# Emission sorted by replayed time, and clock fillers on the spare columns of a score bank

## The chip, the core and the metric

The kernel runs on one core of one Trainium2 chip. The metric is the device time of one execution in microseconds (us), from the median of several runs. The core has five engines with a queue each: PE (TensorE, whose weight loads the profile lists as PEld), DVE (VectorE), ACT (ScalarE), POOL (GpSimd) and SP (SyncE, which issues the DMAs here). Each engine works through its own queue in order and waits on semaphores of the others.

## The reference

Thresholded attention over 8 batches and 8 heads (576 tokens, head dimension 64), then a two-layer feed-forward block over the 4608 tokens with a piecewise gate:

```python
scores = scale * np.matmul(q, k.transpose(0, 1, 3, 2))
thresh = np.max(scores, axis=-1, keepdims=True) - tau
scores = np.where(scores >= thresh, scores, -1000000000.0)
scores = scores - np.max(scores, axis=-1, keepdims=True)
attn = np.exp(scores)
attn = attn / (np.sum(attn, axis=-1, keepdims=True) + 1e-09)
attn_out = np.matmul(attn, v)
...
h = x @ w_in
g = np.where(pos, h, np.where(neg, 0.0, (h + beta) ** 2 / (4.0 * beta)))
return g @ w_out
```

`x` is the attention output with the heads side by side, `pos` is h >= 1 and `neg` is h <= -1.

## The kernel before, in words

All matrices are split into a high and a low float16 part, and a product is three matmuls (high x high, high x low, low x high).

The work falls into stages that overlap. The two weight matrices are loaded in 16 pieces each, and every piece is put together from bits on ACT, POOL and DVE (lines 760 to 787). PE squares each piece into the bank `acc` (the "gram" matmuls, line 794); DVE takes the largest value (line 705), PE spreads it over the partitions (line 708), DVE makes the scales (lines 455 to 457 and 713 to 718), and then the pieces are split into their two parts, some with the help of PE (the "conversions", lines 856 and 857, evicted by ACT at line 863 or DVE at line 861). For q and k, ACT takes sums of squares (line 540), PE spreads them (line 548), DVE and POOL make scales (lines 455 to 457, 555, 560) and the parts are written (lines 568 to 581). v of the first batch is turned by PE (line 679) into a score bank and split by ACT and DVE (lines 684 and 688).

A score tile is 128 rows of queries against 576 keys. PE writes it into one of two score tiles `s0`, `s1` (line 981). A score tile has two PSUM banks of 512 float32 columns; 288 columns of each hold scores, and one more a pad. DVE finds the extreme (line 998), ACT takes the exponential (line 1005), DVE masks and sums (line 1019; in the first tiles line 1025), POOL normalizes (line 1037), ACT and POOL write the two parts (lines 1042 and 1045), and a DMA turns them (line 1067). The first two tiles are turned by PE instead (line 1089, evicted by ACT and DVE at lines 1092 and 1095). PE then multiplies with v (line 1145), and ACT and DVE write the result to `x` (lines 1153 and 1157). The feed-forward block is line 1217 (into one of three banks `ph`), its gate on ACT and DVE (lines 1223 to 1240), line 1262 (into `acc`), and the eviction at line 1280.

The order of the work is a table. Every step is recorded as an operation with an engine, a cost, its predecessors and the buffers it takes and uses. `Plan.order` replays the operations in the order of the table `ORDER`, with those costs: an operation starts at the replayed time `o.t`, when its engine is free, its predecessors have ended and a buffer of its pool is free. The replay decides which slot of a pool each operation gets. The operations are then emitted one after another; emission appends the instructions to the queues of their engines, and the framework adds a semaphore wait wherever an instruction touches a tile region or a PSUM bank that an instruction emitted earlier still reads or writes.

Fillers are matmuls of `ones` with `ones` (128 x 128) whose result nobody reads. They are meant for PE's gaps in the replay, up to 200 us of replayed time, in number `WARM[2]` (0.6) of the gap over `WARM[3]` (0.056 us). Before the change, `gaps` walks over the PE operations in emission order. For each gap over `WARM[0]` it looks through the banks (three of `ph`, `acc`, two of `s`) for the one that stays unheld longest after the gap's start, and notes the gap's start, that bank and the length. The emission loop sets a group ahead of the first operation whose replayed time is not before the gap's start. That gives three groups, of 17, 29 and 19 fillers (line 1296), all on `ph` banks.

Of the kernel before, what the change touches and what calls it, by code (L numbers as in the profile page):

```python
# [18 lines left out]
P = 128  # L19
# [10 lines left out]


EXPM = 0x7F000000
WARM = (1.0, 200, 0.6, 0.056)

LOAD, WLOAD = (0.82, 0.75, 1.8), (1.3, 1.28, 2.0)
QMOVE, KMOVE = (0.33, 0.33, 1.35), (0.64, 0.62, 1.35)
# [243 lines left out]
class Plan:  # L280
# [38 lines left out]
    def order(self):  # L319

        free = {p: [(0.0, x) for x in v] for p, v in self.free.items()}
        idle, dma, mode, self.held = dict.fromkeys(self.HOP, 0.0), 0.0, 0, []
        for o in self.ops:
            o.t = 0.0
        for o in (self.ops[n] for n in ORDER):
            t = max(o.t, idle[o.eng], dma - self.QUEUE if o.eng == "SP" else 0.0)
            for b in o.take:
                x = min(free[b.pool], key=lambda f: f[0])
                free[b.pool].remove(x)
                b.slot, b.end = x[1], 0.0  # L330
                t = max(t, x[0])
            o.t = t
            for b in o.take:
                b.since = t
            end = idle[o.eng] = t + o.cost + (self.TURN if o.eng == "PE" and o.mode != mode else 0.0)
            if o.eng == "PE":
                mode = o.mode
            if o.work:
                dma = max(dma + o.work[0], end + o.work[1])
                end = dma + o.work[2]  # L340
            if o.gives:
                free[o.gives[0]] += [(end + self.FREE, x) for x in o.gives[1]]
            for b in o.uses:
                b.users -= 1
                b.end = max(b.end, end)
                if not b.users:
                    free[b.pool].append((b.end + self.FREE, b.slot))
                    self.held.append((b.pool, b.slot, b.since, b.end))
            for x in o.next:
                x.t = max(x.t, end + (self.HOP[o.eng] if x.eng != o.eng else 0.0))  # L350
            for x in o.behind:
                x.t = max(x.t, t)
        return [self.ops[n] for n in ORDER]


@with_exitstack
def attn_ffn_kernel(ctx: ExitStack, tc: tile.TileContext, qT, kT, vT, tau, w_in, w_out, out):
# [21 lines left out]
    V, A, G, T, Y = nc.vector, nc.scalar, nc.gpsimd, nc.tensor, nc.sync  # L379

    plan = Plan()
# [8 lines left out]
    s_ps = [pp.tile([P, 2, 512], F32, name=f"s{i}") for i in range(2)]  # L390
    plan.pool("ph", 3)
    ph = [pp.tile([P, 512], F32, name=f"ph{i}") for i in range(3)]
    plan.pool("acc", 1)
    accs = [pp.tile([P, 512], F32, name="acc")]
# [32 lines left out]
    ones = cp.tile([P, P], BF16, name="ones")  # L427
# [503 lines left out]
    for b in range(B):  # L931
        s, f, wi, wo = scs[:, b, :], fcs[:, b], wsc["i"], wsc["o"]
# [248 lines left out]
    def wide(g):  # L1181
        return g >= WIDE and len(groups[g]) == 1
# [4 lines left out]
    for g, c0 in [(g, c0) for g in range(NG) for c0 in range(0, gtok[g], GN if wide(g) else P)]:  # L1187
        n = GN if wide(g) else P
# [5 lines left out]
        for fc in range(0, NFC, k):  # L1194
# [49 lines left out]
            o = plan.op("PE", 12 * k * (n / 2400 + 0.0027), ffn1, xdone[g, c0] + xdone.get((g, c0 + n - P), []) + wi, take=[hb, qs[1]], uses=[xbuf[g]])  # L1244
            o = plan.op("ACT", 0.685 + 0.295 * (m - 1), relu, [o] + [fscale[b] for b in bs], take=[tb], uses=[hb])
            o = plan.op("ACT", 0.525, square, [o], uses=[tb])
            o = plan.op("DVE", 0.665 + 0.263 * (m - 1), gate, [o], uses=[tb, hb])
            o = plan.op("ACT", 0.718 + 0.285 * (m - 1), ghi, [o], take=[qs[0]], uses=[hb, qs[1]])
            o = plan.op("DVE", 0.788 + 0.248 * (m - 1), glo, [o], uses=[hb, *qs])
            steps.append((fc, qs, gv, [o] + wo))  # L1250
        for t0 in range(0, n, P):
            if t0:
                ab = plan.buf("acc")
            head, o, left = None, [], [len(steps)]
# [27 lines left out]
            o = plan.op("ACT", 0.575, evict, o + [mo] + [oscale[b] for b in bs], take=[ob], uses=[ab])  # L1282
# [5 lines left out]

                plan.op("SP", 0.55, store, [o], uses=[ob], work=(0.68 * r / P, 0.65 * r / P, 1.05))

    banks = [("ph", x, t[:, :P]) for x, t in enumerate(ph)] + [("acc", 0, accs[0][:, :P])] + [("s", x, t[:, 1, :P]) for x, t in enumerate(s_ps)]

    def keep_warm(bank, us):

        for _ in range(int(us / WARM[3])):
            T.matmul(bank, ones, ones, start=True, stop=True)

    def gaps(order):

        found, free = [], 6.0  # L1300
        for o in order:
            if o.eng != "PE":
                continue
            if o.t - free > WARM[0] and o.t < WARM[1]:
                best = max(((min([t0 for p, x, t0, t1 in plan.held if (p, x) == (pool, n) and t1 > free] + [o.t]), n, pool) for pool, n, _ in banks))
                if best[0] > free + 0.5:
                    us = min(WARM[2] * (o.t - free), best[0] - free)
                    found += [(free, bank, us) for pool, n, bank in banks if (pool, n) == best[2:0:-1]]
            free = max(free, o.t + o.cost)
        return found  # L1310

    with tc.manual_schedule():
        order = plan.order()
        left = gaps(order)
        for o in order:
            while left and left[0][0] <= o.t:
                keep_warm(*left.pop(0)[1:])
            o.fn()


# [28 lines left out]
```

## Time and profile before

| | |
|---|---|
| median of 3 runs | 1137.23 us (1134.74 to 1139.1) |
| profiled execution | 1136.63 us |
| its span on the core | 1134.9 us |
| mean granted PE clock | 0.986 |
| busy: PE, DVE, ACT, POOL | 1093.8, 897.4, 870.1, 790.8 us |
| fillers (line 1296) | 65 matmuls, from 7.8 to 30.6 us |

The span is measured from the first to the last instruction of the profiled execution. Busy time counts an instruction from its start to its end, and matmuls overlap, so a busy PE is not a PE at its peak. The granted clock is the share of full speed that the chip's throttle allows PE. In a row of the timeline stand the start, the length, the engine, line and operation, what it writes and reads, how often, and in brackets how long the engine stood idle before it and who released it.

### The profile page before, as it was taken

How to read it: one execution, taken by the hardware profiler on the slowest of the kernel's cores; microseconds unless marked ns; L12 is line 12 of the kernel's file. 1: busy time of each engine (PE TensorE's matmuls, PEld its weight loads, DVE VectorE, ACT ScalarE, POOL GpSimd, SP SyncE). 2: the span in 40 equal slices, each digit the busy share in tenths (PEclk: the TensorE clock that was granted, in tenths of full speed). 3: DMA queues.
4: the chain of work that ended last, by engine and by line, in shares of the span. 5: the costliest groups of instructions: out<-in, count | busy, mean ns of one | idle time of the engine just before them, and what ended most of it. 6: DMA issues, size and time to landing. Idle time of an engine off the chain costs nothing.

```text
span 1134.9 us, 27108 instructions
## 1 busy us (share of the span) xinstructions
PE 1093.8 (96%) x9461; PEld 761.5 (67%) x9461; DVE 897.4 (79%) x2704; ACT 870.1 (77%) x1676; POOL 790.8 (70%) x904
## 2 busy tenths in 40 slices
PE   5889989999999999999999999999999999999998
PEld 4547657766677676776677667676767677676674
DVE  4899989888799898798879897797769788785231
ACT  6899768878688789778877788677879877686352
POOL 5889997766776898679765886767787875655000
PEclk9689999999999999999999999999999999999999
DMA  8888799779969999669955999659796878555000
GB/s 309 304 223 174 148 198 188 150 133 183 204 123 164 182 194 235 131 133 205 209 113 105 169 203 203 121 110 194 162 198 140 179 149 139 102 100 101 20 11 19
DMA packets 435929, 179.40 MB, mean 158 GB/s; under 512 B 400464, under 2 KB 407632, under 8 KB 435792
## 3 DMA queue, kind: packets, MB, share of 16 engines
q1 hardware_dynamic: 435792, 177.67, 75.9%
q8 instruction: 74, 1.21, 0.4%
q14 instruction: 63, 0.52, 0.1%
HBM read 45.09 MB, written 9.44 MB: 48 GB/s over the span
## 4 chain that ended last, share of the span: by engine, by line
PE 72%; POOL 7%; DVE 7%; ACT 4%; DMA 4%; issue 3%; SPq 1%; DVEq 0%; POOLq 0%; ACTq 0%
PE acc L1262 27%; PE ph L1217 26%; PE s L981 9%; PE ph L1145 7%; POOL hl L1045 3%; POOL e L1037 2%; DMA eT<-hl 2%; DVE e L1019 2%; DVE s L998 2%; DMA raw<-in_k_dram 1%; ACT e L1005 1%; PE ph L856 1%; ACT hl L1042 1%; DMA WO<-in_moe_w_in_dram 1%; POOL nat L581 0%
## 5 line engine op out<-in xcount | busy, mean ns | idle before, releaser
L1045 POOL TENSOR_TENSOR hl<-e,hl 128x576 f16<-128x576 f32 x285 | 366.6, 1293 | 111.1 <-ACT hl L1042 102.9
L1217 PE MATMUL ph<-x,WI 128*128 128x256 f16 (+1 forms) x4032 | 398.9, 257 | 2.0 <-DVE WI L1240 0.9
L1217 PEld LDWEIGHTS <-WI 128*128 128x128 f16 x4032 | 346.4, 98 | 50.0 <-issue 6.1
L1037 POOL TENSOR_SCALAR e<-e,sm 128x576 f32<-128x576 f32 x285 | 220.2, 777 | 102.3 <-DVE sm L1029 71.4
L998 DVE TENSOR_SCALAR_CACHE_REDUCE s<-s,pc 128x576 f32<-128x576 f32 x288 | 232.4, 819 | 61.3 <-PE s L981 60.4
L1005 ACT ACTIVATE e<-s,sm 128x576 f32<-128x576 f32 x288 | 212.0, 741 | 71.4 <-DVE s L998 47.9
L1019 DVE SCALAR_TENSOR_TENSOR e<-s,sm,e 128x578 f32<-128x578 f32 x285 | 230.4, 815 | 30.8 <-ACT e L1005 26.0
L1042 ACT ACTIVATE hl<-e 128x576 f16<-128x576 f32 x285 | 193.3, 682 | 48.8 <-POOL e L1037 38.9
L981 PE MATMUL s<-kk,qq 128*128 128x288 f16 (+3 forms) x1360 | 190.9, 289 | 12.4 <-DVE e L1019 6.7
L1262 PE MATMUL acc<-WO,ga 128*128 128x512 f16 x864 | 202.3, 379 | 0.0
L981 PEld LDWEIGHTS <-qq 128*128 128x128 f16 (+3 forms) x1360 | 113.2, 100 | 76.0 <-issue 34.5
L1230 DVE SCALAR_TENSOR_TENSOR ph<-ph,fcs,asq 128x512 f32<-128x512 f32 (+1 forms) x160 | 111.9, 700 | 58.4 <-ACT asq L1226 57.3
L1223 ACT ACTIVATE asq<-ph,fcs 128x512 f32<-128x512 f32 (+1 forms) x160 | 115.7, 735 | 50.9 <-PE ph L1217 50.1
L1262 PEld LDWEIGHTS <-ga 128*128 128x128 f16 x864 | 82.6, 98 | 85.9 <-issue 2.4
L1145 PE MATMUL ph<-eT,vst 128*64 128x320 f16 (+2 forms) x1928 | 123.1, 279 | 5.6 <-ACT WI L863 2.5
L1145 PEld LDWEIGHTS <-vst 128*64 128x64 f16 x1928 | 98.9, 110 | 28.1 <-issue 18.9
L1240 DVE SCALAR_TENSOR_TENSOR ga<-ph,fcs,ga 128x256 f16<-128x256 f32 (+1 forms) x160 | 70.8, 451 | 31.4 <-ACT gb L1235 14.0
L1226 ACT ACTIVATE asq<-asq 128x512 f32<-128x512 f32 x144 | 90.7, 630 | 2.1
L1235 ACT ACTIVATE ga<-ph,fcs 128x256 f16<-128x256 f32 (+1 forms) x160 | 70.5, 451 | 27.7 <-DVE ph L1230 24.8
L1262 PE MATMUL acc<-WO,gb 128*128 128x512 f16 x300 | 72.8, 379 | 0.0
L1262 PE MATMUL acc<-WO,WI 128*128 128x512 f16 x288 | 67.3, 379 | 0.0
L1262 PE MATMUL acc<-WO 128*128 128x512 f16 x276 | 66.9, 379 | 0.0
(185 smaller groups left out, 1138.5 us busy)
## 6 DMA issues: line engine op xcount, KB each, us to landing
kk<-nat SPq DMA_DIRECT2D x112, 144.0 KB, 3.0
raw<-in_v_dram SPq DMA_DIRECT2D x32, 288.0 KB, 3.5
raw<-in_q_dram SPq DMA_DIRECT2D x32, 288.0 KB, 3.7
raw<-in_k_dram SPq DMA_DIRECT2D x32, 288.0 KB, 3.9
WO<-in_moe_w_in_dram SPq DMA_DIRECT2D x16, 512.0 KB, 7.6
out_dram<-ob SPq DMA_DIRECT2D x32, 256.0 KB, 2.6
qq<-nat SPq DMA_DIRECT2D x112, 72.0 KB, 2.3
x<-in_moe_w_out_dram SPq DMA_DIRECT2D x10, 512.0 KB, 5.3
```

The source lines that it names most:

```text
L981: T.matmul(ap(s, s_ps)[r, f, :SH], q, k, start=ql == kl == 0, stop=kl == 1)
L998: V.tensor_scalar(sv(), sv(), c[:, 24 + v : 25 + v], None, ALU.mult, ALU.min, accum_out=t[:, 0:1])
L1005: A.activation(ev(), sv(), AF.Exp, bias=ap(m, sm)[:, 0:1], scale=-1.0)
L1019: V.scalar_tensor_tensor(ev(SH + 1), sv(SH + 1), t[:, 2:3], ev(SH + 1), ALU.is_le, ALU.mult, accum_out=t[:, 3:4])
L1037: G.tensor_scalar(ev(), ev(), ap(m, sm)[:, 5:6], ESC, ALU.mult, ALU.mult)
L1042: A.activation(part2(0), ev(), AF.Copy)
L1045: G.tensor_tensor(part2(w), ev(), part2(0), ALU.subtract)
L1145: T.matmul(o[hd * D : (hd + 1) * D, :n], vt[:, k, hd * D : (hd + 1) * D], t[:, kb, hd * n : (hd + 1) * n], start=m == 0, stop=m == len(blo ...
L1217: T.matmul(h[:, i], WTh["i"][:, u, wl * 512 + c * P : wl * 512 + (c + 1) * P], x[:, cc, xl, c0 : c0 + n].rearrange("p (t n) -> p t n", n=P ...
L1223: A.activation(tv()[:, :, c], hv()[:, :, c], AF.Relu, bias=fcs[:, b, q, 2 : 3], scale=fcs[:, b, q, 1 : 2])
L1230: V.scalar_tensor_tensor(hv()[:, :, c], hv()[:, :, c], fcs[:, b, q, 0 : 1], tv()[:, :, c], ALU.max, ALU.min)
L1262: T.matmul(ap(ab, accs), gv(h, gl)[:, x], WTh["o"][:, fc + i, wl * 512 : (wl + 1) * 512], start=fc + i == 0 and m == 0, stop=not left[0] a ...
```

## The change

Three things are changed. The replayed list is returned sorted by replayed time (a stable sort). Fillers no longer look for a free bank: all of them write columns 384 to 511 of the second bank of score tile `s0`, which no score, pad or turned tile uses. And the shortest gap that gets fillers is 0.5 us of replayed time instead of 1.0; a group now stands directly ahead of the PE operation that ends the gap, not at the gap's start.

```diff
-WARM = (1.0, 200, 0.6, 0.056)
+WARM = (0.5, 200, 0.6, 0.056)
...
-        return [self.ops[n] for n in ORDER]
+        return sorted((self.ops[n] for n in ORDER), key=lambda o: o.t)
...
-    banks = [("ph", x, t[:, :P]) for x, t in enumerate(ph)] + [("acc", 0, accs[0][:, :P])] + [("s", x, t[:, 1, :P]) for x, t in enumerate(s_ps)]
-
-    def keep_warm(bank, us):
+    spare = s_ps[0][:, 1, 3 * P :]
+
+    def keep_warm(us):
 
         for _ in range(int(us / WARM[3])):
-            T.matmul(bank, ones, ones, start=True, stop=True)
-
-    def gaps(order):
-
-        found, free = [], 6.0
-        for o in order:
-            if o.eng != "PE":
-                continue
-            if o.t - free > WARM[0] and o.t < WARM[1]:
-                best = max(((min([t0 for p, x, t0, t1 in plan.held if (p, x) == (pool, n) and t1 > free] + [o.t]), n, pool) for pool, n, _ in banks))
-                if best[0] > free + 0.5:
-                    us = min(WARM[2] * (o.t - free), best[0] - free)
-                    found += [(free, bank, us) for pool, n, bank in banks if (pool, n) == best[2:0:-1]]
-            free = max(free, o.t + o.cost)
-        return found
+            T.matmul(spare, ones, ones, start=True, stop=True)
 
     with tc.manual_schedule():
         order = plan.order()
-        left = gaps(order)
+        free = 6.0
         for o in order:
-            while left and left[0][0] <= o.t:
-                keep_warm(*left.pop(0)[1:])
+            if o.eng == "PE":
+                if o.t - free > WARM[0] and o.t < WARM[1]:
+                    keep_warm(WARM[2] * (o.t - free))
+                free = max(free, o.t + o.cost)
             o.fn()
```

The bookkeeping of `self.held` and `b.since`, which only `gaps` read, goes too. Lines behind it move up by three, so that line 981 of before is 978 now; the filler is line 1293.

What this does to the queues can be read from the built programs. On DVE, ACT, POOL and SP the same instructions stand in the same order as before: on one engine the replayed times rise along the table anyway. On PE everything but the fillers keeps its order. There are now 13 groups with 172 fillers, and in 10 of them the first filler waits for ACT or DVE, by the count of the semaphore for the last reader of `s0` that was emitted before it.

The first place is PE's queue between the turning of v and the first score tile. Here `s_61` is `s0`, `s_62` is `s1`, `ph_64` is a `ph` bank; a wait names the semaphore of the engine waited for. Before, on PE:

```order
L679 MATMUL s_62<-dgw_132,raw_72 64x128
L1296 LDWEIGHTS ones
L1296 MATMUL ph_64<-ones 128x128
...
L981 LDWEIGHTS qq_82 [waits Activation_49]
L981 MATMUL s_61<-kk_78,qq_82 128x288 [waits DVE_49]
```

And now, on PE:

```order
L676 MATMUL s_62<-dgw_132,raw_72 64x128
L1293 LDWEIGHTS ones
L1293 MATMUL s_61<-ones 128x128 [waits DVE_49]
...
L978 LDWEIGHTS qq_82 [waits Activation_49]
L978 MATMUL s_61<-kk_78,qq_82 128x288
```

The group has 29 fillers in both. The wait for DVE (line 688, the last reader of `s0`) stood at the scores and stands at the first filler now. The next group of before, 19 fillers behind the second score tile, is not there any more.

The second place is PE's queue behind that, at the gram matmuls of the weights. Before, on PE:

```order
L548 LDWEIGHTS sel
L548 MATMUL ph_65<-pc_118,sel 128x2
L794 LDWEIGHTS WI
L794 MATMUL acc<-WI 128x128
...
L794 LDWEIGHTS WI [waits DVE_49]
```

And now, on PE:

```order
L545 MATMUL ph_65<-pc_118,sel 128x2
L791 LDWEIGHTS WI
L791 MATMUL acc<-WI 128x128
...
L1293 LDWEIGHTS ones
L1293 MATMUL s_61<-ones 128x128 [waits DVE_49]
...
L791 LDWEIGHTS WI
```

Behind the first four grams there are now 21 fillers, whose first one waits for DVE's line 1025 on the first score tile; then come eight grams, 9 fillers, four grams and 10 fillers ahead of line 708. The third place is PE's queue at the first product with v. Before, on PE:

```order
L857 MATMUL ph_63<-WI,minus 128x512 [waits Pool_49]
L794 LDWEIGHTS WO [waits DMAHW6_49,DVE_49]
L794 MATMUL acc<-WO 128x128
...
L1145 LDWEIGHTS vst_89
L1145 MATMUL ph_63<-eT_98,vst_89 64x128 [waits Activation_49]
```

And now, on PE:

```order
L854 MATMUL ph_63<-WI,minus 128x512 [waits Pool_49]
L791 LDWEIGHTS WO [waits DMAHW6_49,DVE_49]
L791 MATMUL acc<-WO 128x128
...
L1293 LDWEIGHTS ones
L1293 MATMUL s_61<-ones 128x128 [waits Activation_49]
...
L1142 LDWEIGHTS vst_89
L1142 MATMUL ph_63<-eT_98,vst_89 64x128
```

17 fillers stand between the grams and the product, and wait for ACT's exponential of line 1005 on `s0`. DVE's mask on that tile, emitted later, waits for the last of these fillers. The other groups, in order: 17 at the start as before; 6 ahead of the first line 708; 7 and 6 around the score tile at 44 us; 27 between the grams at 46.5 and 49.2 us, waiting for ACT's line 1005; 9 ahead of the scores at 54.3 us; 5 ahead of those at 68.1 us, for which a mask on DVE waits; and 9 ahead of the conversion at 71.6 us, waiting for DVE's line 998.

More of the change, by code (lines that the diff above doesn't have):

```diff
@@ L321, in order @@
         free = {p: [(0.0, x) for x in v] for p, v in self.free.items()}
-        idle, dma, mode, self.held = dict.fromkeys(self.HOP, 0.0), 0.0, 0, []
+        idle, dma, mode = dict.fromkeys(self.HOP, 0.0), 0.0, 0
         for o in self.ops:
@@ L332, in order @@
             o.t = t
-            for b in o.take:
-                b.since = t
             end = idle[o.eng] = t + o.cost + (self.TURN if o.eng == "PE" and o.mode != mode else 0.0)
@@ L347, in order @@
                     free[b.pool].append((b.end + self.FREE, b.slot))
-                    self.held.append((b.pool, b.slot, b.since, b.end))
             for x in o.next:
```

## The prediction

> **What bounds the kernel now.** I read the page first, then the table of busy times by stretch, and then the timeline of each engine over the first 80 us, because the fillers stand nowhere else.
>
> ```profile
> span 1134.9 us, 27108 instructions
> PEclk9689999999999999999999999999999999999999
> 120.00:140.00 20.00, 18.83 (x202) 12.80 (x201) 18.51 (x52) 15.80 (x29) 19.71 (x22) 1.00 0.82 167
> 300.00:500.00 200.00, 200.00 (x1755) 142.22 (x1753) 175.46 (x543) 164.58 (x324) 151.93 (x161) 1.00 0.88 170
> ```
>
> The columns of the last two rows are the stretch, its length, the busy time of PE, PEld, DVE, ACT and POOL, the granted clock, the DMA share and GB/s. From 300 us PE has no gap at all. Between 120 and 140 us POOL is busy 19.71 of 20 and DVE 18.51, so there the attention tiles set the pace. A late start is therefore not made good later: before 200 us the vector engines are full, after it PE is. The whole effect of the change is how many microseconds the state at about 75 us is reached earlier or later.
>
> In the first 70 us PE waits often and its clock falls. These rows are the same table on a grid of 3.41 us, on which the clock changes:
>
> ```profile
> 20.35:23.77 3.42, 0.79 (x15) 0.71 (x12) 2.46 (x11) 3.33 (x10) 1.70 (x3) 1.00 1.02 361
> 27.18:30.59 3.41, 3.41 (x26) 2.58 (x25) 2.37 (x9) 1.52 (x2) 2.76 (x6) 0.50 0.91 288
> 44.25:47.66 3.41, 1.58 (x20) 1.08 (x16) 3.04 (x12) 3.41 (x8) 3.14 (x5) 1.00 0.30 117
> 47.66:51.07 3.41, 1.86 (x6) 1.00 (x7) 3.27 (x18) 3.41 (x8) 3.07 (x9) 0.50 0.28 40
> 54.49:57.90 3.41, 2.57 (x19) 1.44 (x18) 3.23 (x8) 3.41 (x7) 3.41 (x5) 1.00 1.04 413
> 57.90:61.31 3.41, 1.74 (x36) 1.35 (x35) 3.28 (x10) 3.41 (x8) 3.28 (x4) 1.00 0.80 276
> 61.31:64.73 3.42, 3.21 (x14) 1.72 (x13) 3.38 (x12) 3.42 (x8) 3.37 (x5) 0.50 1.12 285
> ```
>
> A stretch at clock 1.00 with PE busy 0.79, 1.58 or 1.74 is followed by one at 0.50; one with 2.57 is not. Busy for all of 27.18 to 30.59 did not bring the clock back, so a return is not assured.
>
> **Part one: a wait goes.** Before, the second and third filler group write a `ph` bank, and readers of that bank wait for them.
>
> ```profile
> 17.57 0.47 DVE L688 TENSOR_TENSOR vst<-s,vst 64x128 f16<-64x128 f32 x2
> 19.35 1.79 PE L1296 MATMUL ph<-ones 128*128 128x128 bf16 x29
> 21.18 0.16 DVE L455 TENSOR_SCALAR wsc_i<-ph 128x1 f32<-128x1 f32 x1 [3.14 <-PE ph L1296]
> 24.73 0.67 DVE L688 TENSOR_TENSOR vst<-s,vst 128x512 f16<-128x512 f32 x1
> 25.46 1.59 PE L981 MATMUL s<-kk,qq 64*128 64x288 f16 x6 [4.32 <-DVE vst L688]
> 27.16 1.62 PE L981 MATMUL s<-kk,qq 64*128 64x288 f16 x6
> 28.71 2.21 PE L1296 MATMUL ph<-ones 128*128 128x128 bf16 x19
> 31.01 0.17 DVE L455 TENSOR_SCALAR ph<-ph 128x6 f32<-128x6 f32 x1 [1.06 <-PE ph L548]
> ```
>
> Without the wait of 3.14 us DVE does L455 at 18.1, right behind the L688 that ends at 18.04, and L688 at 24.73 - 3.1 = 21.6, done at 22.3. What is late next is the filler itself: the 29 now wait for this L688 (they share its bank) and stand in front of the scores. At 1.79 / 29 = 62 ns each they last until 24.2, to 24.5 if the clock falls at 23.8. The scores start at 24.5 instead of 25.46: 1.0 us gained of 3.1. The group of 19 is gone, so L548, which stood behind its 2.21 us, comes right after the second scores (27.16 + 1.62 - 1.0) and is done at 28.0, and the DVE's L455 moves from 31.01 to 29.05, behind its own order: 2.0 us gained.
>
> **Part two: short gaps are filled where the wait ends last.** The replay puts a group directly ahead of the matmul that ends the gap, and by then a reader of the score bank has mostly been emitted, so the group waits for that reader and runs after the gap, not in it. The first such group:
>
> ```profile
> 32.30 0.81 DVE L1025 SCALAR_TENSOR_TENSOR e<-s,sm,e 128x576 f32<-128x576 f32 x1
> 32.44 1.03 PE L794 MATMUL acc<-WI 128*128 128x128 bf16 x8 [1.01 <-DVE WI L781]
> 33.77 0.61 PE L794 MATMUL acc<-WI 128*128 128x128 bf16 x4 [0.30 <-DVE WI L781]
> 34.63 0.27 DVE L705 TENSOR_REDUCE ssq_i<-acc 128x1 f32<-128x128 f32 x1
> 44.51 0.83 DVE L998 TENSOR_SCALAR_CACHE_REDUCE s<-s,pc 128x576 f32<-128x576 f32 x1 [0.43 <-PE s L981]
> ```
>
> 21 fillers wait for L1025, which ends at 33.11 - 2.0 = 31.1. At half clock a filler costs (2.21 - 0.31) / 18 = 0.106 us (0.31 is the last one's own length, an estimate from the row of 19). Then: 21 fillers 2.2, eight grams 0.9, 9 fillers 1.0, four grams 0.6, sum 4.7, end 35.9. DVE's L705 needs the last gram: 35.9 instead of 34.63. The 2.0 us gained are gone and DVE is **1.3 late**. Behind it DVE is busy until the gap of 0.43 at 44.51, which it eats together with about 0.1 of small ones: **0.7 late**. The groups of 10, 7 and 6 end before DVE asks for what stands behind them; uncovered they would cost their own 0.4 to 1.1 us each.
>
> The second place:
>
> ```profile
> 46.51 0.39 PE L794 MATMUL acc<-WI 128*128 128x128 bf16 x4
> 48.69 0.75 ACT L1005 ACTIVATE e<-s,sm 128x576 f32<-128x576 f32 x1
> 49.21 0.61 PE L794 MATMUL acc<-WI 128*128 128x128 bf16 x4 [2.32 <-DVE WI L783]
> 50.14 0.29 DVE L705 TENSOR_REDUCE ssq_i<-acc 128x1 f32<-128x128 f32 x1
> 54.44 0.60 ACT L863 ACTIVATE WI<-ph 128x512 f16<-128x512 f32 x1 [0.68 <-PE ph L857]
> ```
>
> 27 fillers wait for ACT's L1005, which has slack and ends at about 49.3. They take 27 x 0.062 = 1.7 or 27 x 0.106 = 2.9 us, so L794 starts at 51.0 to 52.2 and L705 at 51.6 to 52.8: DVE is **1.5 to 2.7 late**; I take 1.9, since the grid says the clock holds until 51.07 if PE is busy over half of 44.25 to 47.66, and it is (2.1 us of 3.41 by the moved times). ACT, which here waits 0.68 for PE, ends up 1.2 late.
>
> The third place is the dearest:
>
> ```profile
> 56.67 0.39 PE L794 MATMUL acc<-WO 128*128 128x128 bf16 x4
> 59.41 0.74 ACT L1005 ACTIVATE e<-s,sm 128x576 f32<-128x576 f32 x1
> 59.57 1.03 PE L1145 MATMUL ph<-eT,vst 128*64 128x128 f16 x30 [2.51 <-ACT WI L863]
> 60.53 0.91 PE L981 MATMUL s<-kk,qq 64*128 64x288 f16 x6
> 62.51 0.81 DVE L998 TENSOR_SCALAR_CACHE_REDUCE s<-s,pc 128x576 f32<-128x576 f32 x1
> ```
>
> 17 fillers wait for L1005: 60.15 + 1.2 = 61.35. PE has then idled 2.5 us, and in the stretch that ends at 61.31 it was busy under 1.2 us, so the clock is at half: 17 x 0.106 = 1.8, L1145 starts at 63.2 (3.6 late) and takes about 1.7 instead of 1.03, the scores 1.6 instead of 0.91 (six scores took 1.59 at 25.46, at half clock): end 66.5, where DVE's L998 had 62.51. **4.0 late.**
>
> ```profile
> 67.35 0.82 DVE L1019 SCALAR_TENSOR_TENSOR e<-s,sm,e 128x578 f32<-128x578 f32 x1 [0.86 <-ACT e L1005]
> 67.54 0.63 PE L857 MATMUL ph<-WI,minus 128*128 128x512 f16 x1
> 69.06 0.82 DVE L998 TENSOR_SCALAR_CACHE_REDUCE s<-s,pc 128x576 f32<-128x576 f32 x1 [0.88 <-PE s L981]
> 71.49 0.81 DVE L998 TENSOR_SCALAR_CACHE_REDUCE s<-s,pc 128x576 f32<-128x576 f32 x1
> 71.62 1.12 PE L856 MATMUL ph<-WI,dgw 128*128 128x512 f32 x2 [0.97 <-DVE WO L783]
> ```
>
> DVE's L1019 now waits for 5 fillers that stand behind L857; whether that adds 1 or nothing depends on the clock of the conversions ahead of it. DVE's gap of 0.88 at 69.06 takes some back. The last 9 fillers wait for L998 (72.30) and hold L856 from 71.62 to 72.30 + 0.06 + 9 x 0.062 = 72.9, 1.3 us more on PE and on ACT's conversion behind it, about half of it hidden. **Sum at 75 us: 2.9 late if the clock is back at 68.1, 5.5 if at 71.6; I take 4.0.** No other queue is reordered: the order shows DVE, ACT, POOL and SP row for row as before, so the sort by itself costs nothing.
>
> On the clock, the Trainium skill (TensorE: Matmul & The Clock Gate, section "Why this matters for your kernels") says that only idle gaps over about 3 us send the clock back to half. The trace disagrees: 44.25 to 47.66 has no idle gap over 1.1 us inside it and yet the next stretch has 0.50. What the rule would make of this case is the third rival.
>
> **The rivals.** *Slower by more than can be measured away.* The mechanism is the one place at 59.57, with the clock as its price: if the clock is at half from 47.7 already (PE busy under half of the stretch before), the 27 fillers cost 2.9, ACT's L1005 is 1.8 late, and if the half-row scores (64*128 in the rows) do not bring the clock back until 71.6, the two pairs of L856 between 63 and 68 take twice the 1.12 that the row at 71.62 has. Sum 4.0 + 0.6 + 2.2 = 6.8, of which DVE's gap of 0.88 hides some 0.3: 6.5, 1143.7. For it: 27.18 to 30.59 was full and stayed at 0.50. Against: the fillers use the whole array (128*128). It decides from 5.7 us on.
>
> *Given back later.* The 4 us are taken out of waits between 76 and 160 us, for instance where transposes land late. Then +0.5, 1137.7. Against it stands POOL with 19.71 of 20.
>
> *The clock stays full.* All new gaps are under 3.0 us (19.4 to 22.4 the longest), so the fillers could hold the clock at 1.00 from 13.5 on. Then the scores, grams and fillers up to 35 us run at full speed and L705 comes at 32.7, 1.9 early; the 27 fillers give back 1.1, the 17 fillers 1.0 on PE; the conversions at 63 to 68, twice as fast, win 2 x 1.1. What 68 us then shows is a DVE about 2 early: 1135.2. It needs the stretch 20.35 to 23.77 to survive with 1.4 us busy of 3.42. By the rule of the Trainium skill that is named above it would be this one.
>
> *Nothing.* Fillers with no reader pending would be free, but the order shows a wait on 10 of the 13 groups, so this is only a tail of the third.
>
> **How the numbers follow.** The profiled execution took 1136.63 us, 0.6 under the median of the three runs (1137.23). 1136.63 + 4.0 = 1140.6; against the median 1141.2. Chances: this forecast 0.50, slower rival 0.24, given back 0.13, clock full 0.13. A measurement of this kernel can tell about 0.5%, 5.7 us, from no change. Slower by more: the 0.24 and a tail of 0.03 of the forecast; faster by more: a tail of 0.05 of the clock case, where every filler is hidden; the rest, 0.68, is no difference. The range reaches from just below the clock case (1135.2), at 1134.5, into the slower rival (1143.7), to 1145.
>
> **What would show it.** Right: 172 fillers; the DVE's idle of 3.14 us at L455 gone; scores before 25 us; then DVE idle of about 3 us ahead of L705 near 33 to 36; PE idle before fillers instead of before L794, L1145 and L856; the state that DVE has at 75 us reached 3 to 5 us later, and PE without gaps from 300 us as before. Wrong: a granted clock of 1.00 through 23.8 to 68, fillers that start before their reader ends, or a delay at 75 us that is gone at 200.

## The result, and the profile after

| | before | changed |
|---|---|---|
| median | 1137.82 us (16 runs) | 1141.23 us (16 runs) |
| ratio | | 1.0032, 95% interval 1.0021 to 1.0043 |
| profiled execution, its span | 1136.63, 1134.9 us | 1146.05, 1144.2 us |

The changed kernel is 3.6 us slower (2.4 to 4.9), which is inside the 0.5% that the prediction took as no difference, and its median is 0.03 us from the 1141.2 forecast. The interval is narrower than that bound and does not hold 1. The profiled execution of the changed kernel was the slowest of its 16, so its end can't be compared with the median. Its first 80 us are those of one execution too: a second profile of the same kernel, further down, is 3.6 us away from them at 75 us. Two single executions in the experiments took 1880 us (no filler) and 4832 us (short gaps unfilled, again) and are left out of the ratios.

Two lines of the page of the changed kernel:

```profile
span 1144.2 us, 27324 instructions
...
PEclk9789989999999999999999999999999999999999
```

The clock is lowest in the second and third slice (29 to 86 us), as before, and is down once more in the sixth (143 to 172 us), where it is not before; the last section shows what happened there. The table of busy times, over the stretch that is bound by PE:

```profile
300.00:1100.00 800.00, 797.95 (x6770) 560.36 (x6768) 637.51 (x1918) 615.88 (x1184) 555.66 (x595) 1.00 0.78 150
```

PE is busy 797.95 of 800 us there, as before: nothing that is late at 300 us can be made good. The queues differ in the first 75 us alone, so the places to look at are there. What PE waits for ahead of the filler line, and who waits for the fillers (idle us, times):

```profile
L1293 PE MATMUL s<-ones x172: 216/311/314, 8.5 to 75.2; 128*128 128x128 bf16 x172
...
  ACT e L1002: 5.4, 3
  DVE vst L685: 2.8, 1
  DVE e L1022: 2.6, 1
  DVE s L995: 1.0, 1
  DVE eT L1092: 0.9, 1
...
  DVE e L1016: 1.1, 1
```

The first row is the filler, then come the releasers: in seven places PE stood still ahead of a filler, 12.7 us together. The last row is the other direction: DVE's L1016 waited 1.1 us for fillers. The timeline of PE, at the places that the prediction priced:

```profile
22.39 2.29 PE L1293 MATMUL s<-ones 128*128 128x128 bf16 x29 [2.79 <-DVE vst L685]
24.62 1.62 PE L978 MATMUL s<-kk,qq 64*128 64x288 f16 x6
...
31.20 2.40 PE L1293 MATMUL s<-ones 128*128 128x128 bf16 x21 [2.61 <-DVE e L1022]
33.39 1.06 PE L791 MATMUL acc<-WI 128*128 128x128 bf16 x8
...
49.07 3.04 PE L1293 MATMUL s<-ones 128*128 128x128 bf16 x27 [1.77 <-ACT e L1002]
51.90 0.63 PE L791 MATMUL acc<-WI 128*128 128x128 bf16 x4
...
61.97 1.97 PE L1293 MATMUL s<-ones 128*128 128x128 bf16 x17 [3.13 <-ACT e L1002]
63.87 1.81 PE L1142 MATMUL ph<-eT,vst 128*64 128x128 f16 x30
...
74.75 0.66 PE L1293 MATMUL s<-ones 128*128 128x128 bf16 x9 [1.02 <-DVE s L995]
75.25 1.08 PE L853 MATMUL ph<-WI,dgw 128*128 128x512 f32 x2
```

And the timeline of DVE, which waits for what stands behind the fillers:

```profile
18.20 0.14 DVE L452 TENSOR_SCALAR wsc_i<-ph 128x1 f32<-128x1 f32 x1
...
29.05 0.16 DVE L452 TENSOR_SCALAR ph<-ph 128x6 f32<-128x6 f32 x1
...
35.87 0.29 DVE L702 TENSOR_REDUCE ssq_i<-acc 128x1 f32<-128x128 f32 x1 [3.13 <-PE acc L791]
...
52.57 0.29 DVE L702 TENSOR_REDUCE ssq_i<-acc 128x1 f32<-128x128 f32 x1 [1.81 <-PE acc L791]
...
63.98 0.82 DVE L1016 SCALAR_TENSOR_TENSOR e<-s,sm,e 128x578 f32<-128x578 f32 x1 [1.08 <-PE s L1293]
...
67.36 0.83 DVE L995 TENSOR_SCALAR_CACHE_REDUCE s<-s,pc 128x576 f32<-128x576 f32 x1 [0.94 <-POOL e L1034]
```

DVE's waits of 3.13, 1.81 and 1.08 us in these brackets are new, and the one of 3.14 us at the first L455 of before is gone (L452 at 18.20). The matmuls at a gap's end now start when a reader of `s0` is done and the fillers have run, not when their own operands are there. Against the same instruction of before DVE is 2.0 us early at 29 us, 1.2 late at 35.9, 0.5 late at 45, 2.4 at 52, 4.9 at 67 and 3.4 from 75 to 85.

### The profile page after: what moved, and what is told of

It is laid out like the page before. It is cut to its first block, busy times and chain, and to the rows that moved or that the text cites. A ratio compares the mean times of both kernels' runs of the same rounds, so it can differ in the third digit from the quotient of the medians.

```text
span 1144.2 us, 27324 instructions
## 1 busy us (share of the span) xinstructions
PE 1101.6 (96%) x9568; PEld 770.3 (67%) x9568; DVE 900.2 (79%) x2704; ACT 870.4 (76%) x1676; POOL 790.0 (69%) x904
## 4 chain that ended last, share of the span: by engine, by line
PE 66%; DVE 11%; ACT 7%; POOL 6%; issue 4%; DMA 4%; SPq 1%; DVEq 0%; ACTq 0%; POOLq 0%
PE acc L1259 24%; PE ph L1214 24%; PE s L978 9%; PE ph L1142 7%; DVE s L995 3%; POOL hl L1042 3%; DVE e L1016 2%; POOL e L1034 2%; ACT e L1002 1%; ACT hl L1039 1%; DMA eT<-hl 1%; DMA raw<-in_v_dram 1%; PE s L1293 1%; ACT asq L1220 1%; DVE ph L1227 1%
## 5 line engine op out<-in xcount | busy, mean ns | idle before, releaser
L995 DVE TENSOR_SCALAR_CACHE_REDUCE s<-s,pc 128x576 f32<-128x576 f32 x288 | 232.5, 819 | 61.9 <-PE s L978 59.6
L1016 DVE SCALAR_TENSOR_TENSOR e<-s,sm,e 128x578 f32<-128x578 f32 x285 | 230.6, 815 | 35.4 <-ACT e L1002 29.0
L1220 ACT ACTIVATE asq<-ph,fcs 128x512 f32<-128x512 f32 (+1 forms) x160 | 115.7, 735 | 50.3 <-PE ph L1214 49.5
L1142 PE MATMUL ph<-eT,vst 128*64 128x320 f16 (+2 forms) x1928 | 124.4, 281 | 3.5 <-DMA eT<-hl 1.4
L1142 PEld LDWEIGHTS <-vst 128*64 128x64 f16 x1928 | 99.1, 111 | 27.0 <-issue 16.6
```

The costliest lines, as they stand in the source:

```text
L995: V.tensor_scalar(sv(), sv(), c[:, 24 + v : 25 + v], None, ALU.mult, ALU.min, accum_out=t[:, 0:1])
L1016: V.scalar_tensor_tensor(ev(SH + 1), sv(SH + 1), t[:, 2:3], ev(SH + 1), ALU.is_le, ALU.mult, accum_out=t[:, 3:4])
L1142: T.matmul(o[hd * D : (hd + 1) * D, :n], vt[:, k, hd * D : (hd + 1) * D], t[:, kb, hd * n : (hd + 1) * n], start=m == 0, stop=m == len(blo ...
L1220: A.activation(tv()[:, :, c], hv()[:, :, c], AF.Relu, bias=fcs[:, b, q, 2 : 3], scale=fcs[:, b, q, 1 : 2])
```

## The experiments

Theory W is the prediction's: the cost is in groups that wait for a late reader of `s0` and then run on the path. Its rivals are that the number of fillers costs, that the clock is worth more than the waits, and that the sort itself does something. Each kernel computes all of the reference. "DVE at 75 us" is the start of the same instruction against the profile of before, in one execution; the ratio is of many.

That column holds also what came ahead of the first place. The first rise to full clock in the profiles comes between 11.3 and 17.0 us (a filler or gram takes 0.31 us ahead of it and 0.22 behind it). At 17.4 us DVE is already 1.5 to 1.8 us late against before in the three profiles with the rise at 15.8, 16.9 and 17.0 us (no filler, sorted list alone, one filler a group), and 0.7 us early where it comes at 11.3 (without 29). Counted from there, DVE at 75 us is 6.7 us early without fillers, 6.0 with the groups at the gap's start, 4.5 in the sorted list alone, and 3.2 and 0.1 late in the two profiles of the changed kernel.

| kernel | fillers | DVE at 75 us | ratio, 95% interval |
|---|---|---|---|
| no filler (second) | 0 | -4.9 | 0.9972 (0.9958 to 0.9985) |
| one filler a group | 13 | -2.9 | 0.9979 (0.9965 to 0.9992) |
| groups of 17 and 29 | 46 | -4.6 | 0.9990 (0.9976 to 1.0003) |
| without 21, 27, 17 | 107 | -0.5 | 1.0014 (0.9999 to 1.003) |
| without 29 | 143 | -0.1 | 0.9999 (0.9987 to 1.0011) |
| short gaps unfilled | 111 | -0.5 | 1.0053 (1.0038 to 1.0067) |
| the same again | 111 | +1.1 | 1.0025 (1.0011 to 1.0039) |
| changed | 172 | +3.4 | 1.0032 (1.0021 to 1.0043) |
| changed again | 172 | -0.2 | 1.0026 (1.0014 to 1.0038) |
| 21, 27, 17 doubled | 237 | +4.8 | 1.0070 (1.0044 to 1.0096) |
| changed, at gap's start | 172 | -6.4 | 0.9971 (0.9959 to 0.9983) |
| sorted list alone | 65 | -2.9 | 0.9965 (0.9951 to 0.9979) |
| sorted, 0.5 us, bank search | 121 | -4.4 | 0.9965 (0.9952 to 0.9978) |

**The sorted list alone**, in the kernel before:

```diff
-        return [self.ops[n] for n in ORDER]
+        return sorted((self.ops[n] for n in ORDER), key=lambda o: o.t)
```

> Before, with the sorted list alone: the bank search, the threshold of 1.0 and the three groups of 17, 29 and 19 stay. DVE, ACT, POOL and SP have the same rows, but the groups move on PE: an operation whose replayed time is not before the gap's start now comes later in the list, so the group of 29 stands behind DVE's L455 in the emission and waits for it, instead of L455 waiting for the fillers, and the group of 19 goes from ahead of L548 to between the grams. Theory A, as the prediction has it ("the sort by itself costs nothing"): no difference, ratio 1.000. Theory B (a filler's place against the readers of its bank is what counts, and the sort moves it): DVE's wait of 3.14 us at L455 is gone, DVE 3 us early at 18 to 26 us and about 4 early at the first L705 (30.6 instead of 34.6), of which 2 to 3.5 are left at 75 us: 2 to 3.5 us faster, ratio 0.997 to 0.998.

Measured 0.9965: 4 us faster than before, near the numbers of theory B (0.997 to 0.998), and not 1.000. The timeline of PE in this kernel:

```profile
20.86 1.79 PE L1296 MATMUL ph<-ones 128*128 128x128 bf16 x29
...
26.48 1.22 PE L1296 MATMUL ph<-ones 128*128 128x128 bf16 x19
```

and DVE's reader of the bank, which had waited 3.14 us for the 29, now without a bracket:

```profile
19.47 0.14 DVE L455 TENSOR_SCALAR wsc_i<-ph 128x1 f32<-128x1 f32 x1
...
30.98 0.27 DVE L705 TENSOR_REDUCE ssq_i<-acc 128x1 f32<-128x128 f32 x1
```

The 29 fillers lie in the gap and nobody waits for them, nor they for anybody. The first L705 starts at 30.98 instead of 34.63. So in the kernel before, the sort alone takes away the wait that the prediction credited to the new bank. That the sort moves nothing but fillers can be read from the built programs: the kernel without fillers has the same rows on all five queues with the sorted list and with the table's own order.

**No filler at all**, in the changed kernel:

```diff
-WARM = (0.5, 200, 0.6, 0.056)
+WARM = (0.5, 0, 0.6, 0.056)
```

> The changed kernel with no filler at all (it still computes everything). Theory W (what costs 3.4 us is where fillers wait for readers of s0): all these waits go, and the removed wait at L455 stays removed: 1 to 3 us faster than before, ratio 0.997 to 0.999, so 4 to 6 us faster than the changed kernel. Rival C (the clock is worth more than the waits: without fillers it is at half until 68 us or later): grams, scores and conversions take twice as long in the first 70 us, DVE at 75 us 3 us or more late against before, ratio 1.003 or above. The granted clock between 13 and 68 us tells which.

Measured 0.9972: 3.2 us faster than before and 6.8 us below the changed kernel's 1.0032. This is theory W. Rival C falls, although the clock did what it says: rows of the table of busy times on this execution's own clock grid (PE's busy time first, the granted clock third from the end):

```profile
22.59:26.00 3.41, 1.97 (x11) 1.03 (x11) 3.11 (x7) 3.32 (x9) 3.33 (x5) 0.50 0.94 247
...
32.83:36.24 3.41, 3.41 (x12) 1.92 (x12) 3.14 (x16) 2.98 (x5) 3.15 (x6) 0.50 1.03 407
...
43.07:46.48 3.41, 1.47 (x14) 1.20 (x13) 3.15 (x20) 3.41 (x7) 3.06 (x7) 0.50 0.17 70
46.48:49.90 3.42, 3.42 (x8) 1.41 (x7) 3.24 (x18) 2.81 (x6) 3.25 (x7) 0.50 0.84 277
...
56.72:60.14 3.42, 3.42 (x22) 2.17 (x18) 3.34 (x14) 3.42 (x9) 3.23 (x5) 0.50 1.67 247
60.14:63.55 3.41, 3.41 (x5) 1.07 (x5) 2.55 (x9) 2.46 (x5) 3.41 (x5) 0.50 0.55 155
```

Eight stretches between 22 and 64 us, 27.3 us together, are at half clock, and DVE is busy 2.55 to 3.34 of 3.41 in the six that are shown: PE at half speed still delivers nearly in time here.

**The three groups doubled, and left out**, in the changed kernel (2 in the first, 0 in the second):

```diff
+                    for _ in range(2 if group in (3, 8, 10) else 1):
-                    keep_warm(WARM[2] * (o.t - free))
+                        keep_warm(WARM[2] * (o.t - free))
+                    group += 1
```

> The changed kernel with the groups of 21, 27 and 17 doubled to 42, 54 and 34, the other ten as they are. Theory W (these three run after their gap, on the path): 21 x 0.114 + 27 x 0.09 + 17 x 0.116 = 2.4 + 2.4 + 2.0 = 6.8 us more on PE, of which 4 to 6 reach DVE at 75 us: 4 to 6 us slower than the changed kernel, 7.5 to 9.5 slower than before, ratio 1.0065 to 1.0085; if the added fillers hold the clock at full through 47 to 54 us, 2 less. Rival F (fillers lie in PE's idle time and their number is free): as the changed kernel, ratio 1.003.

> The changed kernel without the groups of 21, 27 and 17; the other ten groups (107 fillers, 29 of them in the group at 19 us) stay. Theory W: the three shifts of DVE that the profile shows behind them (from -1.97 to +1.32 at 35 us, +0.5 to +2.4 at 50 us, +2.2 to +4 at 63 us) go, and what is left is the gain of 2 at 31 us less the small groups: 0 to 2 us faster than before, ratio 0.998 to 1.000. Rival C (these fillers held the clock, so leaving them out costs as much as it saves): ratio 1.003 as the changed kernel, with a clock at half for longer than 23.5 to 37.1, 47.4 to 54.2 and 61.0 to 67.9 us.

Doubled: 1.0070, 8 us slower than before and 4.3 above the changed kernel, as theory W has it, so their number is not free. PE's timeline of the doubled kernel:

```profile
30.32 4.64 PE L1293 MATMUL s<-ones 128*128 128x128 bf16 x42 [3.16 <-DVE e L1022]
...
49.37 5.92 PE L1293 MATMUL s<-ones 128*128 128x128 bf16 x54 [1.77 <-ACT e L1002]
...
64.13 2.06 PE L1293 MATMUL s<-ones 128*128 128x128 bf16 x34 [3.05 <-ACT e L1002]
```

The waits are those of the single groups within 0.6 us. The first two run 2.2 and 2.9 us longer; the third only 0.1, because its 34 run at full clock, where the 17 of the changed kernel ran at half. Left out: 1.0014, between the two theories. It is 1.6 us slower than before where theory W had 0 to 2 faster, and its interval overlaps that of the changed kernel: the 2 us that leaving them out takes off are not clear of the noise. Something among the other ten groups costs some 4.8 us against no fillers (0.9972). The first suspicion fell on the short groups.

**Short gaps unfilled**, in the changed kernel:

```diff
-WARM = (0.5, 200, 0.6, 0.056)
+WARM = (1.0, 200, 0.6, 0.056)
```

> The changed kernel with the threshold back at 1.0 us of replayed gap: of its 13 groups only those of 17, 29, 21, 27 and 17 stay, on the spare columns of s0 and at the gap's end. Theory W (a filler costs where it waits for a reader of s0, the dear groups are 21, 27 and 17): the eight short groups are worth little, so 2 to 3.5 us slower than before, ratio 1.0015 to 1.003. Theory M (each of the small groups costs too, which the run without the three dear ones suggests: at 75 us it was 0.5 early where the kernel without fillers was 4.9 early): the short groups go with what they cost, half a us to 3 us faster than the changed kernel, ratio 1.000 to 1.002.

Measured 1.0053 (6 runs), above every number expected: without the short groups the kernel was not faster. Its profile (DVE 0.5 early at 75 us) is of the fastest of the six, 1137.62 us, and explains nothing about the others. It was run again below.

**The groups at the gap's start**, in the changed kernel:

```diff
-        free = 6.0
+        free, left = 6.0, []
...
-                    keep_warm(WARM[2] * (o.t - free))
+                    left.append((free, WARM[2] * (o.t - free)))
                 free = max(free, o.t + o.cost)
+        for o in order:
+            while left and left[0][0] <= o.t:
+                keep_warm(left.pop(0)[1])
             o.fn()
```

> The changed kernel with each group emitted at its gap's start instead of ahead of the operation that ends the gap: same 172 fillers, same bank columns. The group of 27 then waits for nobody, the groups of 21 and 17 wait for earlier readers, and some readers (L995, L1002, L1016) wait for fillers instead. Theory W (what counts is whether a group runs in its gap or after it): most of the cost goes, at 75 us DVE is between 3 early and 1 late against before, ratio 0.998 to 1.001. Rival L (172 fillers on PE cost by their number and load, wherever they stand): as the changed kernel, ratio 1.003.

Measured 0.9971, 7 us below the changed kernel with the same 172 fillers in the same columns. The same three groups in PE's timeline:

```profile
25.41 2.24 PE L1293 MATMUL s<-ones 128*128 128x128 bf16 x21 [0.72 <-ACT e L1002]
...
41.39 1.67 PE L1293 MATMUL s<-ones 128*128 128x128 bf16 x27
...
53.27 1.11 PE L1293 MATMUL s<-ones 128*128 128x128 bf16 x17
```

Two of them wait for nobody and the third 0.72 us instead of 2.61, and DVE's L702 starts at 30.09 without a wait, where the changed kernel has 35.87 after 3.13. In turn DVE and ACT wait for fillers in three places, 2.8 us together. Rival L falls. This run also holds the clock best, at half for 6.8 us in two stretches (25.6 to 29.1 and 46.1 to 49.5), and is no faster than the kernel without fillers at 27.3 us of half clock.

**Sorted list, threshold of 0.5 us, bank search kept** (the kernel before with two lines changed):

```diff
-WARM = (1.0, 200, 0.6, 0.056)
+WARM = (0.5, 200, 0.6, 0.056)
...
-        return [self.ops[n] for n in ORDER]
+        return sorted((self.ops[n] for n in ORDER), key=lambda o: o.t)
```

> Before with the sorted list and the threshold of 0.5 us, but with the search for a bank that stays free and the groups at the gap's start: ten groups (17, 6, 29, 19, 9, 10, 7, 6, 9, 9), whose waits are for readers that are long done. Theory W: fillers that wait for no late reader cost nothing, so it is as the sorted list alone (0.9965), ratio 0.996 to 0.998. Theory M (small groups cost what their own length is, wherever the gap in the trace is not the gap in the replay): 1 to 3 us slower than the sorted list alone, ratio 0.9975 to 0.9995.

Measured 0.9965, as the sorted list alone: no filler here waits for a reader or is waited for, and 121 of them cost nothing that can be told. These two have the lowest ratio of all, 4 us below before and 7.6 below the changed kernel; their intervals overlap those of the kernels without fillers and with the groups at the gap's start.

**One filler in each group**, in the changed kernel:

```diff
-        for _ in range(int(us / WARM[3])):
+        for _ in range(min(1, int(us / WARM[3]))):
```

> The changed kernel with one filler in each of its 13 groups, so that every wait for a reader of s0 stands where it stood and the running time of the fillers is gone. If the waits themselves are what costs (PE held until the reader is done): as the changed kernel, ratio 1.003. If the running time behind the waits is what costs (21 x 0.114, 27 x 0.09, 17 x 0.116 and the rest): near the kernel without fillers, 1 to 3.5 us faster than before, ratio 0.997 to 0.999; the wait alone should hold the grams behind the first one by some 0.7 us, those at 49 us by 0.3 and L1142 by 0.6, of which 1 to 1.5 us reach 75 us.

Measured 0.9979. In the queues all waits stand as in the changed kernel; its PE timeline:

```profile
30.77 0.26 PE L1293 MATMUL s<-ones 128*128 128x128 bf16 x1 [2.60 <-DVE e L1022]
...
45.72 0.27 PE L1293 MATMUL s<-ones 128*128 128x128 bf16 x1 [1.77 <-ACT e L1002]
...
57.16 0.22 PE L1293 MATMUL s<-ones 128*128 128x128 bf16 x1 [3.15 <-ACT e L1002]
```

The waits of 2.60, 1.77 and 3.15 us cost at most a little (0.9979 against 0.9972 without fillers, intervals that overlap), because PE would have stood idle for nearly as long anyway: without fillers it waits 1.88, 1.92 and 2.42 us at these three places, for its own operands. What costs is the running time that comes behind the wait.

**The groups of 17 and 29 alone, and all but the 29**, in the changed kernel. The two conditions in the loop of the doubled kernel are `1 if group in (0, 2) else 0` and `0 if group == 2 else 1`.

> The changed kernel with its first group (17, at the start) and the group of 29 in front of the first scores alone; the eleven later groups are left out. The kernel without the groups of 21, 27 and 17 came out at 1.0014, the one without any filler at 0.9972, so the ten that stayed cost some 4.8 us together. Theory G29 (the group of 29 is most of that: it keeps the first scores back by 2 us): near 1.000 to 1.0015. Theory S (the eight short groups are most of it, each its own length): 0.9975 to 0.9985.

> The changed kernel without the group of 29; the twelve others stay. Theory G29: 2 to 4 us faster than the changed kernel, ratio 0.9995 to 1.0015. Theory S: 1 us faster at most, ratio 1.0025 to 1.0035. Rival C (the 29 hold the clock over 20 to 24 us, so without them grams and the 21 fillers run at half from 20 us on): slower than the changed kernel, 1.004 or more.

Alone 0.9990, all but the 29 0.9999; the changed kernel, measured beside them, 1.0026. Leaving out the 29 takes 3.1 us off the changed kernel, and the intervals do not overlap: theory G29, and rival C (1.004 or more) is out. It is the group whose 29 fillers wait for L685 and keep the first scores back. From the other side, 0.9972 to 0.9990, the two groups alone cost 2 us, with overlapping intervals. Theory S is out for the run without the 29. The kernel with two groups does not decide: 0.9990 lies between the numbers of the two theories, and its interval reaches into both.

**The changed kernel and the one with short gaps unfilled, again**, on one chip.

> The changed kernel once more, on the chip of the run below, because the kernel without the short groups came out at 1.0053 on another chip, above the 1.0032 of the changed kernel. No theory wants a difference from 1.0032 here. The profile should have no instruction of 6 us on line 649; then its shift at the end is the +3.4 to +4.8 of 75 to 145 us and not +9.

> The kernel with the threshold back at 1.0 (groups of 17, 29, 21, 27 and 17) once more, beside the changed kernel. Theory C (the short groups hold the clock in some windows, which is worth more than their own length): 1.5 to 3 us slower than the changed kernel beside it, and a profile in which the clock is at half for more windows between 13 and 68 us than in that of the changed kernel. Theory M (the first profile of this kernel, 0.5 early at 75 us, is the usual one and the slow times came from that chip): within 1 us of the changed kernel or faster.

Measured 1.0026 and 1.0025: no difference, so theory C of the short groups is not borne out, and the 1.0053 was not repeated. Why that run came out higher stays open; so does the worth of the short groups within 2 us either way.

What this repeat showed beyond that is how much one program varies. The changed kernel's second profile (1137.94 us, the fastest of its 12, where the first is the slowest of its 16) has DVE 0.2 early at 75 us, where the first has it 3.4 late. DVE's distance between the two is 0.6 us at 34 us, 1.4 behind the 21 fillers, 1.6 behind the 27, 2.2 at 56 us and 3.6 behind the 17; it is 4.2 from 94 to 148 us. The last step, in the second profile: PE's timeline at the 17 fillers, and the table of busy times on this execution's own clock grid:

```profile
59.45 1.11 PE L1293 MATMUL s<-ones 128*128 128x128 bf16 x17 [3.07 <-ACT e L1002]
```

```profile
57.30:60.71 3.41, 1.26 (x25) 1.16 (x26) 3.33 (x11) 3.19 (x6) 3.33 (x4) 1.00 0.68 230
60.71:64.12 3.41, 3.41 (x43) 2.26 (x38) 2.35 (x11) 1.94 (x5) 3.31 (x5) 0.50 1.38 241
64.12:67.54 3.42, 2.85 (x16) 1.38 (x15) 3.38 (x10) 3.42 (x7) 2.20 (x4) 1.00 0.93 242
```

and the same table of the first profile:

```profile
57.61:61.02 3.41, 1.23 (x7) 0.46 (x6) 3.41 (x8) 3.41 (x7) 2.43 (x3) 1.00 0.63 237
61.02:64.44 3.42, 2.47 (x29) 2.27 (x30) 2.26 (x9) 1.98 (x4) 3.23 (x5) 0.50 0.83 277
64.44:67.85 3.41, 3.41 (x39) 2.28 (x36) 1.95 (x8) 2.10 (x6) 2.56 (x3) 0.50 1.31 112
```

In the second profile the 17 fillers run just ahead of the fall at 60.71, in 1.11 us, and the stretch at half clock behind them is full; the clock is back at 64.12. In the first they start at 61.97, behind the fall at 61.02, and take 1.97 us; the stretch has 2.47 us of work, and half clock goes on until 67.85. So the same 17 fillers on the path take 1.97 or 1.11 us, by where the grid lies.

## Why the prediction was right, point by point

*What bounds the kernel.* Right in that a delay is not made good: the two profiles of the changed kernel are 3.6 us apart at 75 us, 4.2 before one instruction at 148 us (last section), 9.2 behind it and 8.1 at the end. But "The whole effect" is not settled at 75 us. In each of the other 13 profiles DVE ends later against before than it was at 75 us, by 0.4 (sorted, 0.5 us, bank search) to 5.9 us: without fillers it is 4.9 early at 75 us and 1.9 at the end, and with the groups of 17 and 29 alone it goes from 4.6 early to 1.4 late. The forecast has nothing for this. The profile of before is 1.2 us below the median of its kernel, which may be part of it; no experiment here explains the rest.

*Part one.* The times came as worked out: L452 at 18.20 (18.1 predicted), scores at 24.62 (24.5), L452 at 29.05 (29.05). The 29 fillers in front of the scores were the reason that only 1.0 of 3.1 us was to be gained. That price, 2.1, is 2.2 in the profile (from 22.39 to 24.62), and the run without them is 3.1 us faster.

*The sort.* "No other queue is reordered ... so the sort by itself costs nothing": right for the changed kernel, as far as the built programs tell. There a group stands directly ahead of a PE operation, and PE's order is the same without the sort; built without it, the changed kernel has the same instructions in the same order, and only a few waits around the groups of 7 and 6, at 44 us, differ. No run has it. What the prediction passed over is the kernel before, where groups stand by replayed time: there the sort gains 4 us alone. So the wait of 3.14 us goes with either of the two, by the run with the sort alone and by that built program. The 7.6 us between the sorted list alone and the changed kernel (0.9965 to 1.0032) come from the place at the gap's end, behind late readers: with the groups at the gap's start the same columns cost nothing that can be told (0.9971).

*The 21 fillers.* DVE's L702 at 35.87 (35.9 predicted), 1.2 late (1.3); at 45 us 0.5 late (0.7).

*The 27 fillers.* "The grid says the clock holds until 51.07 if PE is busy over half of 44.25 to 47.66, and it is": the busy time was right (2.14 us of that stretch) and the inference wrong. The rows of the first profile's own grid, and PE's longest wait in the first of them:

```profile
43.96:47.37 3.41, 2.37 (x26) 1.59 (x25) 3.29 (x11) 3.32 (x8) 3.23 (x5) 1.00 0.00 0
47.37:50.78 3.41, 1.71 (x17) 1.71 (x17) 3.20 (x17) 2.62 (x6) 2.98 (x8) 0.50 0.06 7
```

```profile
45.12 0.49 PE L1293 MATMUL s<-ones 128*128 128x128 bf16 x6 [0.93 <-DVE eT L1092]
```

The clock fell at 47.37, after a stretch with 2.37 of 3.41, so half of a stretch is not enough. The prediction's own row of 57.90 to 61.31 spoke against it: 1.74 of 3.41 is over half, and the next stretch is at 0.50. DVE was 2.4 late instead of 1.9, near the 2.7 that the prediction gave for half clock. On the other hand the clock came back at 67.85, the better of the two cases.

*The 17 fillers.* L1142 at 63.87 (63.2), DVE's L995 at 67.36 (66.5): 4.9 late instead of 4.0, the 0.5 of the step before and 0.4 of its own.

*The sum.* 4.0 predicted at 75 us, 3.4 in the first profile, -0.2 in the second; in time 3.6 and 3.0 us by the two ratios. The 4.0 lay between 2.9 for a clock back at 68.1 and 5.5 for one back at 71.6, two numbers given without their terms. The clock was back at 67.85, and DVE went from 4.9 late to 3.4 where that case has 4.0 to 2.9. That the forecast of 1141.2 is met to 0.03 us is luck: the median before turned out 0.6 us higher and the cost some 0.4 lower.

*The rivals.* The clock stayed full in neither profile of the changed kernel. In that rival's sum, "2 x 1.1" is too much: L856 between 63 and 68 us takes 2.01 and 1.92 us before, 0.9 and 0.8 more than 1.12. The slower rival's clock at half from 47.4 came, its clock until 71.6 did not. Of the 10 groups with a wait in the queue, 7 were waited with in fact; the others found their reader done.

On the rule of the Trainium skill (TensorE: Matmul & The Clock Gate, section "Why this matters for your kernels") that idle gaps over about 3 us send the clock down, the rows again show a fall without one: no wait of PE in 43.96 to 47.37 is longer than 0.93 us, and the next stretch is at 0.50. On another statement of that page (section "Part 1: The HAM clock gate (the "warmup" mystery)") they agree: the window is free-running and does not start with the kernel. The two profiles of one program show it, with stretches of 3.41 us that lie differently against the instructions.

## What to carry to other kernels

A filler that writes a bank with live readers is an instruction like any other: if it is emitted behind a late reader, it runs after the gap, and its price is its running time on the path. Place it where its bank's readers are long done (0.9965 here) or at the gap's start (0.9971), or leave it out (0.9972): no version with fillers was shown to beat the one without, and there PE at half clock still delivered nearly in time.

And look at what an edit moves that is placed by time and not by the table; in the kernel before, a sort that changes no row of real work was worth 4 us through the fillers alone. One profile is not enough to tell a few microseconds: two executions of one program were 3.6 us apart at 75 us.

## What the runs showed of the hardware

The clock changes only on a grid of 3.41 us whose place against the program differs from one execution to the next. In the first 85 us of the 14 profiles it fell after 40 of 55 stretches at full clock with PE busy under 2.4 us and held after 153 of 156 with more. But it held after one with 1.42 (the doubled kernel, 62.14 to 65.55) and fell after one with 2.61 (short gaps unfilled, the first time, 23.86 to 27.27), so busy time alone does not decide it.

The first profile of the changed kernel has one instruction that no other profile has. DVE's timeline, and then POOL's, at that place:

```profile
148.53 6.32 DVE L649 SCALAR_TENSOR_TENSOR vb<-raw,scs,vb 128x576 f16<-128x576 f32 x1
```

```profile
148.48 0.77 POOL L565 TENSOR_SCALAR raw<-raw,pc 128x576 f32<-128x576 f32 x1
149.20 0.77 POOL L1034 TENSOR_SCALAR e<-e,sm 128x576 f32<-128x576 f32 x1
...
154.33 1.08 POOL L847 TENSOR_SCALAR WO<-WO,wsc_o 128x512 f16<-128x512 f32 x1
```

The 28 instances of this line take 1.07 us in the median; this one took 6.32, while POOL worked without a gap. In all other profiles the longest took 3.06. DVE's delay against before is 4.5 us at its start, 9.8 right behind it and 9.3 at the end. PE had nothing to do from 153.0 to 156.7 us, and the clock fell at 156.6. The Trainium skill (SBUF — State Buffer, section "Who interferes with whom") says that a DVE instruction with two inputs in SBUF, as this one has, contends with a GpSimd instruction that reads SBUF. The overlap agrees with that; no run here took POOL's work away, so the cause is not shown.
